# A retention layer and token mixer on one core: wq and wk in one product, named PSUM banks, weights later, a new order, smaller store descriptors

## The chip, the cores and the metric

One core of one Trainium2 chip. The metric is device time in microseconds of one execution. The kernel before had a median of 112.32 us in its first three runs (112.2 to 112.54).

A word on states: a run counts as slow when it is over 1.5% above the fastest of the same kernel in its group.

## The reference, cut to what matters

```python
# q, k, v: (4, 8, 768, 64) float32;  w_q, w_k: (512, 64);  w_out: (512, 512)
for t in range(S):                                   # retention, one state per head
    state = gamma * state + k[t] v[t]^T
    y[t] = q[t] . state / sqrt(D)
x = y.transpose(0, 2, 1, 3).reshape(B, S, 512)
W = (x @ w_q) @ (x @ w_k)^T / sqrt(64)               # token mixing without softmax
out = relu(W @ x) @ w_out                            # (4, 768, 512) float32
```

Both kernels cut the sequence into 12 pairs of 128-token chunks (three pairs per batch). Per pair: q and k are multiplied by powers of gamma (`cq`, `ck`), transposed (`trq`, `trk`), scores of two halves are made (`sc`), masked on the way out of PSUM (`eat`), multiplied by v (`ia`), and the inter-chunk part and the running state are added (`X`, `Y`, `st`). Then x is copied (`ex`), transposed (`xt`, `exT`) and multiplied by w_q and w_k (`wqk`). Once a batch's three pairs are there, z = wk^T x (`zm`), the mixing (`mx`), relu (`r`), the output product (`pj`), its copy (`eo`) and the store follow.

## The kernel before

A string gives the order of all steps; the letter names the engine of a copy (A ScalarE, V VectorE, P GpSimd). Each engine runs its own steps in that order.

```python
ORDER = """
fill.80 ck.0:V trk.0 cq.0:V ekT.0:A trq.0 cv.0:V fill.2 eqT.0:V
st.0 es.0.0:A sc.0.0 X.0 eat.0.0:V es.0.1:A sc.0.1 ck.1:P ia.0.0
# ... 39 more lines
"""
at_psum = pool("at_psum", 1, space=PSUM)   # 2 banks: one score tile at a time
y_psum = pool("y_psum", 1, space=PSUM)     # 2 banks
s_psum = pool("s_psum", 1, space=PSUM)     # 1 bank
psum = pool("psum", 3, space=PSUM)         # 3 banks for all else, in turn

for p in range(STAGES):                    # 6 pairs are asked for at the start
    for name in "kqv":
        load(name, p)
    if p == 2:                             # w_q, w_k and w_out (1 MB) behind pair 2
        ...
def wqk(e, p):
    for a in range(NDM):                   # wq, already transposed: 4 products of 256 columns
        nc.tensor.matmul(out=ps[:, 0 : 2 * C]..., lhsT=wq_sb[:, a]..., rhs=st["xT"][:, a]...)
    for c in range(2):
        for a in range(NDM):               # wk: 8 products of 64 columns
            nc.tensor.matmul(out=ps[:, 2 * C + c * DH : ...], lhsT=st["xT"][:, a, c, :], rhs=wk_sb[:, a, :])
```

## Time and profile before

| kernel before, profiled run | |
|---|---|
| span | 109.7 us (time 112.3) |
| TensorE busy, VectorE, ScalarE, GpSimd | 93.8, 64.9, 60.0, 49.4 us |
| start of the first real matmul, last matmul start | 8.7, 104.8 us |
| last output copy to end of span | 4.0 us |
| pauses of TensorE over 0.3 us between 8 us and the last matmul, in sum | 15.3 us |

"Pause" here and below is a distance over 0.3 us between the starts of two successive TensorE instructions, weight loads and matmuls counted alike, taken from the trace's list of instructions. The profile's "busy" row is not used for that, since matmul spans overlap (in the trace of the kernel before an output matmul lasts 380 ns in the mean, and the next one starts 216 ns after it). A position such as "before instruction 961" counts the same list from its start.

### The profile page before, as it was taken

How to read it: one execution, taken by the hardware profiler on the slowest of the kernel's cores; microseconds unless marked ns; L12 is line 12 of the kernel's file. 1: busy time of each engine (PE TensorE's matmuls, PEld its weight loads, DVE VectorE, ACT ScalarE, POOL GpSimd, SP SyncE). 2: the span in 40 equal slices, each digit the busy share in tenths (PEclk: the TensorE clock that was granted, in tenths of full speed). 3: DMA queues.
4: the chain of work that ended last, by engine and by line, in shares of the span. 5: the costliest groups of instructions: out<-in, count | busy, mean ns of one | idle time of the engine just before them, and what ended most of it. 6: DMA issues, size and time to landing. Idle time of an engine off the chain costs nothing.

```text
span 109.7 us, 4707 instructions
## 1 busy us (share of the span) xinstructions
PE 93.8 (85%) x2132; PEld 68.9 (63%) x2132; DVE 64.9 (59%) x87; ACT 60.0 (55%) x94; POOL 49.4 (45%) x41
## 2 busy tenths in 40 slices
PE   3999596994579899999998959999999999958930
PEld 3998485783458576667687837557787647633400
DVE  1066756894422665687688849799857954225100
ACT  5004137265273975958848515549587866554640
POOL 6405968008699996968229999321000000000000
PEclk9999958999967999999999999999999999999999
DMA  1999999999999999999999999824040022430471
GB/s 38 309 347 346 342 342 238 313 334 306 289 327 337 345 344 304 339 337 333 287 297 281 300 354 370 332 115 166 31 197 0 6 87 111 191 158 33 191 312 73
DMA packets 40917, 26.77 MB, mean 244 GB/s; under 512 B 1857, under 2 KB 38721, under 8 KB 40897
## 3 DMA queue, kind: packets, MB, share of 16 engines
q1 hardware_dynamic: 39856, 25.96, 75.0%
q10 hardware_dynamic: 1040, 0.52, 1.6%
q8 instruction: 16, 0.26, 0.9%
q14 instruction: 5, 0.03, 0.1%
HBM read 20.19 MB, written 6.29 MB: 241 GB/s over the span
## 4 chain that ended last, share of the span: by engine, by line
PE 78%; DVE 10%; issue 5%; ACT 3%; POOL 1%; POOLq 0%; DVEq 0%; ACTq 0%
PE o_ps L538 20%; PE at_ps L316 8%; PE y_ps L422 6%; PE ktr_ps L243 6%; PE xt_ps L445 6%; DVE at_sb L329 6%; PE wqk_ps L460 6%; PE qtr_ps L299 6%; PE y_ps L385 5%; PE ktr_ps L285 3%; PE z_ps L492 3%; PE wqk_ps L470 3%; PE mx_ps L514 3%; PE state_ps L385 2%; DVE xT L133 1%
## 5 line engine op out<-in xcount | busy, mean ns | idle before, releaser
L329 DVE TENSOR_TENSOR at_sb<-at_ps,cmask 128x1024 bf16<-128x1024 f32 x24 | 29.3, 1222 | 9.5 <-PE at_ps L316 9.3
L253 POOL TENSOR_TENSOR ks<-k_st,fk 128x1024 bf16<-128x1024 f32 x11 | 20.9, 1902 | 19.0 <-DMA k_st<-in_k_dram 14.8
L538 PE MATMUL o_ps<-wout_sb,relu 128*128 128x512 bf16 x96 | 24.1, 380 | 0.3 <-ACT o_st L132 0.3
L253 POOL TENSOR_TENSOR qs<-q_st,fq 128x1024 bf16<-128x1024 f32 x11 | 20.9, 1902 | 1.2 <-DMA q_st<-in_q_dram 1.2
L132 ACT COPY o_st<-o_ps 128x512 f32<-128x512 f32 x19 | 11.1, 586 | 9.9 <-PE o_ps L538 9.8
L316 PE MATMUL at_ps<-qT,kT 64*64 64x128 bf16 x384 | 10.6, 221 | 4.0 <-DVE at_sb L329 2.3
L538 PEld LDWEIGHTS <-relu 128*128 128x128 bf16 x96 | 8.2, 98 | 8.0 <-issue 1.2
L132 ACT COPY kT<-ktr_ps 128x1024 bf16<-128x1024 bf16 x7 | 7.1, 1015 | 9.9 <-PE ktr_ps L285 9.9
L529 ACT ACTIVATE relu<-mx_ps 128x512 bf16<-128x512 f32 x18 | 10.2, 598 | 3.3 <-PE mx_ps L514 2.6
L316 PEld LDWEIGHTS <-kT 64*64 64x64 bf16 x384 | 7.1, 106 | 6.7 <-issue 5.6
L132 ACT CAST s_sb<-state_ps 128x256 bf16<-128x256 f32 x16 | 6.0, 373 | 8.8 <-PE state_ps L385 8.7
L385 PE MATMUL y_ps<-s_sb,qT 64*64 64x64 bf16 x320 | 9.6, 195 | 1.0 <-DVE at_sb L329 1.0
L133 DVE COPY xT<-xt_ps 128x1024 bf16<-128x1024 bf16 x10 | 6.7, 686 | 6.1 <-PE xt_ps L445 6.1
L385 PEld LDWEIGHTS <-qT 64*64 64x64 bf16 x320 | 7.2, 108 | 4.7 <-issue 2.7
L385 PE MATMUL state_ps<-vs,ks 64*64 64x64 bf16 x320 | 8.9, 194 | 1.5 <-issue 1.4
L422 PE MATMUL y_ps<-vs,at_sb 64*128 64x64 bf16 x384 | 10.0, 193 | 0.2
L243 PEld LDWEIGHTS <-warm 128*128 128x128 bf16 x90 | 7.7, 129 | 1.9 <-DVE warm L174 1.1
L422 PEld LDWEIGHTS <-at_sb 64*128 64x128 bf16 x384 | 7.2, 96 | 2.6 <-DVE at_sb L329 0.5
L132 ACT CAST x_nat<-y_ps 128x1024 bf16<-128x1024 f32 x6 | 6.1, 1012 | 4.7 <-PE y_ps L422 4.6
L243 PE MATMUL ktr_ps<-identity,warm 128*128 128x128 bf16 x80 | 7.0, 275 | 1.9 <-POOL identity masks.py:199 1.9
L385 PEld LDWEIGHTS <-ks 64*64 64x64 bf16 x320 | 6.9, 109 | 2.4 <-issue 2.1
L531 DVE TENSOR_SCALAR relu<-mx_ps 128x512 bf16<-128x512 f32 x6 | 4.2, 692 | 7.1 <-PE mx_ps L514 7.1
(57 smaller groups left out, 137.5 us busy)
## 6 DMA issues: line engine op xcount, KB each, us to landing
q_st<-in_q_dram SPq DMA_DIRECT2D x12, 512.0 KB, 6.7
v_st<-in_v_dram SPq DMA_DIRECT2D x12, 512.0 KB, 6.5
k_st<-in_k_dram SPq DMA_DIRECT2D x11, 512.0 KB, 6.7
out_dram<-o_st SPq DMA_DIRECT2D x11, 512.0 KB, 2.7
wout_stage<-in_moe_w_out_dram SPq DMA_DIRECT2D x1, 1024.0 KB, 7.0
k_st<-in_k_dram ACTq DMA_DIRECT2D x1, 512.0 KB, 5.6
out_dram<-o_st SPq DMA_DIRECT2D x2, 256.0 KB, 2.8
wq_stage<-in_moe_w_q_dram SPq DMA_DIRECT2D x1, 128.0 KB, 5.4
```

What stands on the lines that cost most here:

```text
L132: return nc.scalar.copy(out=out, in_=in_)
L133: return ENGINES[e].tensor_copy(out=out, in_=in_)
L243: nc.tensor.transpose(dst, warm, identity)
L253: ENGINES[e].tensor_tensor(out=st[name + "s"].rearrange("p hp j x d -> p x (hp j) d"), in0=st[name + "_st"].rearrange("p (x hp) j d -> p x ...
L299: nc.tensor.transpose(ps[:, hp, :, j, :], st["qs"][:, hp, j], identity)
L316: nc.tensor.matmul(out=ps[rows(c), x, hi, j, :], lhsT=st["kT"][rows(x), hp, j, c, :], rhs=st["qT"][rows(x), hp, c, :], start=(hi == 0 and ...
L329: st["eat", half] = ENGINES[e].tensor_tensor(out=st["at", half].rearrange("p x hi j t -> p (x hi) (j t)"), in0=st["at_ps", half].rearrange ...
L385: out.append(nc.tensor.matmul(skip_group_check=True, **mm))
L422: nc.tensor.matmul(out=st["y_ps"][:, c, x, hp, :], lhsT=st["at", half][rows(c), x, hi, j, :], rhs=st["vs"][rows(c), hp, j, x, :], start=(( ...
L445: nc.tensor.transpose(ps[:, a, c, :], st["x"][:, c, a * 128 : (a + 1) * 128], identity)
L529: nc.scalar.activation(out=dst, in_=src, func=ACT.Relu)
L538: nc.tensor.matmul(out=ps, lhsT=st["relu"][:, a, j], rhs=wout_sb[:, a, :], start=(a == 0), stop=(a == NDM - 1),)
```

## The change

The intent: less TensorE work in `wqk`; two score tiles at once; pairs 3 to 5 earlier; no stores between loads; an order that fills TensorE's holes; and smaller packets, so that the core's instruction fetches are not held up behind large ones. The last purpose is my reading of it, and b_512b, below, does not bear it out. (The trace of the kernel before lists 16 packets of 16 KB on the instruction queue, q8, beside 4264 weight loads and matmuls: from that, and from the period of 256 in TensorE's stops, I take each packet to bring 256 instructions of TensorE.)

```diff
-for p in range(STAGES): ... load k, q, v; at p == 2: w_q, w_k, w_out
+LOADS = "q0 v0 k1 q1 v1 k2 q2 v2 w k3 q3 v3 k4 q4 v4 k5 q5 v5 o k6 ...".split()
+# k of pair 0 in two halves on two queues; stores only once every load has been issued
-            nc.sync.dma_start(out=dst, in_=pairs[p]["o"])
+            nc.sync.dma_start(out=dst, in_=pairs[p]["o"], max_dma_last_dim=512)
+                out=wout_stage, in_=moe_w_out.rearrange("(p a) m -> p a m", a=NDM), max_dma_last_dim=512
-    at_psum, y_psum, s_psum, psum = four pools
+    banks = psum.tile([128, 8, 512], FP32, name="banks")     # a step names its bank: sc.0.1@4
-    wqk: 4 products of 256 columns (wq) and 8 of 64 (wk)
+        for c in range(2):
+            for a in range(NDM):
+                nc.tensor.matmul(out=ps[:, c, :], lhsT=st["xT"][:, a, c, :], rhs=wqk_sb[:, a, :], ...)
+    ewq, ew: copy wq (twice, side by side) and wk out; tw: transpose wq; ewt: copy it out
-    r: two relus of 512 columns
+    r: one relu of 1024 columns over two banks
-    fill.80 ... (100 fillers of 128 columns)
+    fill.20@6 ... (32 fillers of 512 columns)
+# ORDER is new throughout, with more copies on VectorE; x is laid out so that w_q, w_k and w_out
+# can be loaded "(p a)" instead of "(a p)"
```

## The prediction

> **What bounds the kernel now.** I began with the page: busy times, then the slices.

> ```profile
> PE 93.8 (85%) x2132; PEld 68.9 (63%) x2132; DVE 64.9 (59%) x87; ACT 60.0 (55%) x94; POOL 49.4 (45%) x41
> ...
> PE   3999596994579899999998959999999999958930
> ...
> PEclk9999958999967999999999999999999999999999
> DMA  1999999999999999999999999824040022430471
> ```

> PE is busiest, and from slice 15 (about 40 us) it has hardly a hole. Before that it has holes, two dips of its clock, and a DMA queue that is full until 70 us. The table of busy time by window, cut where the character of the run changes, says the same in numbers (columns: window, its length, PE busy, weight loads, DVE, ACT, POOL, clock, DMA share, GB/s):

> ```profile
> 8.90:40.00 31.10, 24.88 (x629) 19.87 (x625) 18.16 (x21) 16.38 (x24) 22.64 (x14) 0.89 1.08 320
> 40.00:97.00 57.00, 55.20 (x1390) 39.24 (x1388) 41.06 (x50) 36.94 (x59) 23.73 (x14) 1.00 0.68 220
> 97.00:105.80 8.80, 6.69 (x38) 2.67 (x36) 2.77 (x4) 4.99 (x9) 0.00 (x0) 1.00 0.40 163
> ```

> Matmul spans overlap, so "busy" overstates the work. I took start-to-start distances of matmuls at full clock instead: 216 ns for an output matmul (512 columns), 56 for a 128-column transpose, 109 for the 256-column wq product, 29 for the 64-column wk product, 15 to 21 for the 64-row tiles. By counts: outputs 96 x 216 = 20.7 us, transposes 288 x 56 = 16.1, scores 8.1, at@v 7.5, inter and state 9.0, wq/wk 48 x 109 + 96 x 29 = 8.0, z 3.1, mx 3.8: **76.3 us**. From 8.9 to 105.2 us is 96.3. About 54 us of the work lies in 40:97, 7 after, so about 15 us in the 31 us from 8.9 to 40. That is where the time is lost.

> The chain of work that ended last shows how. At 24 us and again at 30 us (start, us, what):

> ```profile
> 25.38 0.29 PE at_ps L316 x11
> 25.67 1.40 issue
> 27.07 0.28 PE at_ps L316 x5
> 27.35 0.02 issue
> 27.37 1.24 DVE at_sb L329
> ...
> 30.54 0.84 PE xt_ps L445 x8
> 31.38 0.02 issue
> 31.40 0.70 DVE xT L133
> 32.10 0.04 issue
> 32.15 1.01 PE wqk_ps L460 x4
> ```

> Three losses are in view. (a) 1.40 us of "issue" in the middle of one score group, 11 of 16 matmuls done: no operand is missing. (b) One score buffer: `at_sb` takes 1.24 us on DVE, and the next score group must wait. (c) Eight transposes take 0.84 us where 0.45 is normal: half clock. The half clock lasted from 13.7 to 17.2 us and from 30.8 to 34.2.

> For (a) I counted the PE's instructions (weight loads and matmuls): it stops before number 961, 2497 and 2753, each 193 past a multiple of 256. An instruction packet of 16 KB ended 1.2 to 1.4 us before each resumption. The three stops cost 1.6 + 0.6 + 1.5 us. [...]the first while the output weights were in flight (2048-byte packets, 84 ns each; loads' 512-byte packets take 27 ns), the third just after the first store (4096-byte packets, 159 ns).

> [...]the two dips are 3.4 us long each, after thin PE work. [...]`at_sb` 1222 ns for 1024, `x_nat` 1221, against 686 for bf16 `xT`.

> ```profile
> L329 DVE TENSOR_TENSOR at_sb<-at_ps,cmask 128x1024 bf16<-128x1024 f32 x24 | 29.3, 1222 | 9.5 <-PE at_ps L316 9.3
> L253 POOL TENSOR_TENSOR ks<-k_st,fk 128x1024 bf16<-128x1024 f32 x11 | 20.9, 1902 | 19.0 <-DMA k_st<-in_k_dram 14.8
> ```

> The second row: POOL waited 14.8 us for loads of k, so the first third is fed by DMA, too.

> **The change part by part.**

> *wq and wk in one product.* 48 x 109 + 96 x 29 = 8.0 us becomes 96 matmuls of 128 columns and 24 transposes, 120 x 56 = 6.7 us: 1.3 us less PE. Evacuation grows from one copy of 384 columns (482 ACT, 555 DVE) to three, about 0.4 + 0.3 + 0.3 us; twelve times 0.5 is 6 us more on ACT and DVE, and one more round trip before mx, off the path except at the end.

> *Explicit banks.* Seven banks are shared by all; scores of one half go to one pair of banks while the other half is masked. Removes loss (b): at 11.1 to 14.1 us alone two `at_sb` of 1.24 us lay in series on the chain. relu becomes one instruction over two banks, about 1.0 us instead of 2 x 0.6.

> *Late weights.* Before, wq, wk and the 1 MB of w_out stand between pair 2 and pair 3. A load of 512 KB takes 1.5 us of the queue, so w_out 3.0: pairs 3 to 5 land 3 us earlier. Stores now come only after the last load; 20.2 MB at 0.34 MB/us end near 62 us rather than 70.

> *Fill.* 100 short filler matmuls become 32 of 512 columns, 20 of them in front: at half clock until about 6.9 us, they end at 8.2. k in halves is cast by then. So the first transpose starts as before (8.7).

> *New order.* I laid the order of each engine out by hand, token by token, up to the second half of pair 6's scores, with the durations above. Result: scores of pair 3 start near 27.4 us against 35.9 (with 1.5 us of z and wq/wk of batch 0 not yet done). At 45.5 us some 28.3 us of PE work are done. The kernel before reaches the same point near 52.4. **Lead 6.9 us**, in which 1.6 of the first fetch stop, 2.5 of half clock and 3 of w_out are contained.

> *Descriptors of 512 bytes.* If packets cause the late fetches, the two stops after 52 us (0.6 and 1.5, at 59.5 and 63.6) go: 2.0 less. Price: 8 x 84 = 0.67 becomes 32 x 27 = 0.86 us per engine for the last store, +0.2.

> *DVE.* Its list sums to 77 us (64.9 before; 24 masks alone 29.3), ACT to 56. By 45.5 us some 37 of these 77 are done, so 40 remain in about 50 us: dense, in order, beside a PE that has 46.7 in the same time. I charge 1.5 us.

> Sum: 112.3 - 6.9 - 0.8 (the rest of the 1.3 on PE) - 2.0 + 0.2 + 1.5 = **104.3 us**. The end itself (last copy 0.6, store 2.8, finish) stays.

> **The rivals.** First: *DVE becomes the bound*. For it: 77 us in about 95, its masks sit between every score and product. Against: ACT has room, and bank pairs let two scores wait. Every wait would turn up as PE idle behind `at_sb`; then the rest runs at 86% (as my layout of 27 to 45 us did), not 90: 107 to 108 us. Second: *instruction fetch bounds a faster PE*. For it: [...]the stop at 59.5 came with no store in flight. Stops then return before 62 us: 1 to 3 us, 106 us. Third: *the head is DMA-fed anyway* and the reorder waits for pairs instead of banks, or the PE goes thin and the clock halves again: gain only 3 in the head, 108 us. Fourth: all works, no DVE loss, order as good to the end: 101 us.

> **Range and chances.** The sum is 104.3; the fourth gives the low side, 100.5; the rivals singly reach 108, which I take as the high side. For "same" the change would have to lose nearly all of 8 us, two rivals together. Faster 0.92, same 0.06, slower 0.02.

> **What would show it.** Right: PE clock at full from about 7 us; scores of pair 3 near 28 us; no "issue" piece over 1 us in the chain after 20 us; PE work 75.0 by start-to-start; no score group waiting for `at_sb` in the first 30 us; the z product of batch 0 near 32 us; DVE near 77 busy; loads ending near 62. Wrong: stops at a fixed place modulo 256 still there (second rival), PE idle behind DVE growing between 45 and 97 us (first), half-clock slices (third), or PE starting later than 9.5 us because of the fillers.

## The result

105.81 us median of four runs (103.83, 104.13, 107.5, 108.59), the kernel before 112.43 in the same group. The ratio of the fast runs is **0.9233** (95% interval 0.9183 to 0.9282). Ratios are the mean time of one kernel's fast runs over that of the other's of the same rounds, so not quite the ratio of the medians quoted. Three later groups with the same kernel on other occasions gave medians of 106.51, 105.69 and 105.89 against 112.16, 111.52 and 112.02: ratios of medians 0.945 to 0.950. The means of their fast runs give 0.967, 0.950 and 0.944, but the first has only one fast run of the kernel before and the last only one of the changed kernel. The ratio of 0.9233 rests on two fast runs; about 5% is the better figure.

The page of the changed kernel, busy times and slices of 2.6 us (a run of the slow label, 105.8 us of span):

```profile
PE 90.7 (86%) x2040; PEld 63.3 (60%) x2040; DVE 77.0 (73%) x108; ACT 54.6 (52%) x87; POOL 46.1 (44%) x41
...
PE   5997986849999996998999699689999999999800
...
PEclk9999999975599999999999999999999999999996
DMA  1999998999999999999999999999133060661993
```

Its table by window, columns as in the prediction:

```profile
8.90:40.00 31.10, 26.99 (x759) 21.69 (x757) 23.93 (x34) 15.35 (x23) 20.21 (x14) 0.89 1.07 318
40.00:97.00 57.00, 52.84 (x1238) 37.01 (x1237) 46.10 (x58) 36.61 (x61) 21.78 (x13) 1.00 0.76 221
97.00:105.80 8.80, 3.23 (x15) 1.26 (x13) 2.99 (x4) 0.99 (x2) 0.00 (x0) 0.91 0.80 240
```

TensorE carries more in the first third (759 matmuls, some fillers among them, instead of 629) and *less* between 40 and 97 us (1238 instead of 1390, since much was done before); it is done about 5 us earlier. VectorE went up by the 12 us foreseen. The DMA queue is full (digits of 8 and 9) until 74 us, before until 71, and full again at the very end (two digits of 9), where before it was not (4 and 7). There is still a stretch of half clock (22.3 to 29.1 us).

Pauses of TensorE over 0.3 us, summed by stretch, in us, and the tail:

| profile | 8 to 30 | 30 to 50 | 50 to 70 | 70 to last matmul | last copy to end | span |
|---|---|---|---|---|---|---|
| before | 6.6 | 2.1 | 3.1 | 3.6 | 3.96 | 109.7 |
| after, first profile | 5.0 | 2.8 | 3.3 | 1.0 | 4.94 | 105.8 |
| after, again (fast label) | 4.3 | 3.6 | 3.0 | 0.6 | 4.95 | 104.7 |

So the time came from the head (about 2 us of pauses) and, unforeseen, from the last stretch (about 3 us); the middle, from 30 to 70 us, has about 1 us more of pauses than before; the tail (last copy to end) grew by 1.0 us. For the fast-label profile: the last matmul starts 6.0 us earlier (98.7 against 104.8); 3.8 of that are fewer pauses, 1.3 by estimate the smaller product, 0.9 the rest. In the rest are, not told apart, a first real matmul at 7.4 instead of 8.7 us and a half clock of 3.4 instead of 6.8 us. The longer tail takes 1.0 back: 5.0 us of span.

Two pauses of the changed kernel show what remains. The timeline of its first profile near 21 us (start, us, engine, line, operation, count, idle before):

```profile
20.57 0.35 PE L333 MATMUL banks<-qT,kT 64*64 64x128 bf16 x10
22.50 0.18 PEld L333 LDWEIGHTS <-kT 64*64 64x64 bf16 x6 [1.73 <-issue]
22.50 0.42 PE L333 MATMUL banks<-qT,kT 64*64 64x128 bf16 x6 [1.57 <-issue]
```

A score group stops after 10 of 16 matmuls, with no wait that the profile shows ("issue"). The stop stands before instruction 705 = 2 x 256 + 193, the same place modulo 256 as in the kernel before; "stop" below means a pause at this place. The half clock begins at 22.3 us, 0.2 us before the stop ends.

The other is at 14 us and is new. The same few instructions in the first profile, where it went well, and in the profile of a_same3, the same kernel, where it went badly:

```profile
13.68 0.68 DVE L127 CAST vs<-v_st 128x1024 bf16<-128x1024 f32 x1
...
14.21 1.91 POOL L263 TENSOR_TENSOR ks<-k_st,fk 128x1024 bf16<-128x1024 f32 x1 [1.05 <-DMA k_st<-in_k_dram]
```

```profile
14.00 1.90 POOL L263 TENSOR_TENSOR ks<-k_st,fk 128x1024 bf16<-128x1024 f32 x1 [0.49 <-DMA k_st<-in_k_dram]
14.02 2.43 DVE L127 CAST vs<-v_st 128x1024 bf16<-128x1024 f32 x1
...
16.50 0.26 PE L399 MATMUL banks<-vs,ks 64*64 64x64 bf16 x2 [1.93 <-DVE vs L127]
```

VectorE's cast of v of pair 1 took 0.68 us where it started before GpSimd's decay (by 0.53 us), and 2.43 us where it started 0.02 us after it; TensorE then waited 1.93 us for it, and the cast ended 0.55 us after GpSimd's operation. Why, the traces do not show. Ten profiles of the changed kernel and its variants have the two side by side. In four the cast starts first and takes 0.68 us, in six it starts 0.02 to 0.69 us later, takes 1.76 to 2.43 us and ends 0.55 us after GpSimd, in each of them. The kernel before had this cast on VectorE only for pair 0, while GpSimd was idle (686 ns). The clock in a_same3 is halved from 16.2 to 23.0 us; that begins in the last 0.35 us of the wait.

### The profile page after: what moved, and what is told of

It is laid out like the page before.

```text
span 105.8 us, 4560 instructions
## 1 busy us (share of the span) xinstructions
PE 90.7 (86%) x2040; PEld 63.3 (60%) x2040; DVE 77.0 (73%) x108; ACT 54.6 (52%) x87; POOL 46.1 (44%) x41
## 5 line engine op out<-in xcount | busy, mean ns | idle before, releaser
L345 DVE TENSOR_TENSOR at_sb<-banks,cmask 128x1024 bf16<-128x1024 f32 x24 | 28.9, 1220 | 7.6 <-PE banks L333 7.4
L263 POOL TENSOR_TENSOR ks<-k_st,fk 128x1024 bf16<-128x1024 f32 (+1 forms) x10 | 18.4, 1841 | 13.7 <-DMA k_st<-in_k_dram 6.5
L569 PE MATMUL banks<-wout_sb,relu 128*128 128x512 bf16 x96 | 23.0, 379 | 1.2 <-DVE wout_sb L127 1.0
L126 ACT CAST x_nat<-banks 128x1024 bf16<-128x1024 f32 x11 | 11.1, 1012 | 8.2 <-PE banks L399 7.4
L126 ACT COPY o_st<-banks 128x512 f32<-128x512 f32 x15 | 8.6, 589 | 9.0 <-PE banks L569 8.9
L333 PE MATMUL banks<-qT,kT 64*64 64x128 bf16 x384 | 10.6, 226 | 3.0 <-issue 1.6
L251 PE MATMUL banks<-warm 128*128 128x512 bf16 x32 | 10.2, 454 | 2.0 <-DVE warm L190 1.2
L399 PE MATMUL banks<-s_sb,qT 64*64 64x64 bf16 x320 | 10.1, 200 | 0.1
L399 PE MATMUL banks<-vs,ks 64*64 64x64 bf16 x320 | 8.8, 194 | 1.3 <-issue 1.1
L436 PE MATMUL banks<-vs,at_sb 64*128 64x64 bf16 x384 | 9.3, 195 | 0.2 <-DVE at_sb L345 0.2
```

The lines of the kernel that those rows point to most:

```text
L126: return nc.scalar.copy(out=out, in_=in_)
L251: nc.tensor.matmul(out=bank32(b), lhsT=warm[:, 0:128], rhs=warm, start=True, stop=True)
L263: ENGINES[e].tensor_tensor(out=st[name + "s"][:, :, :, xs].rearrange("p hp j x d -> p x (hp j) d"), in0=st[name + "_st"][:, xs].rearrange( ...
L333: nc.tensor.matmul(out=ps[rows(c), x, hi, j, :], lhsT=st["kT"][rows(x), hp, j, c, :], rhs=st["qT"][rows(x), hp, c, :], start=(hi == 0 and ...
L345: ENGINES[e].tensor_tensor(out=st["at", half].rearrange("p x hi j t -> p (x hi) (j t)"), in0=st["at_ps", half].rearrange("p (xhi jt) -> p ...
L399: out.append(nc.tensor.matmul(skip_group_check=True, **mm))
```

## The experiments

Twelve runs gave a result, in four groups; nine of them are variants, three the changed kernel again. In each group all kernels shared the runs of the kernel before on the same chip. Medians in us, with the ratio to the median of before:

| run | what | median | before | ratio of medians | stops at the 256-period, us in sum | tail |
|---|---|---|---|---|---|---|
| a_same | changed kernel | 106.51 | 112.16 | 0.950 | 7.7 | 4.95 |
| a_bigst | large stores | 105.37 | 112.16 | 0.940 | 5.2 | 4.33 |
| a_bigall | large stores and w_out | 108.16 | 112.16 | 0.964 | 6.4 | 4.35 |
| a_earlyw | w_out early | 106.48 | 112.16 | 0.949 | 2.3 | 4.95 |
| a_same2 | changed kernel | 105.69 | 111.52 | 0.948 | 6.1 | 4.94 |
| a_halfloads | half the loads | 103.46 | 111.52 | 0.928 | 3.4 | 4.69 |
| a_fly2 | two loads under way | 125.85 | 111.52 | 1.129 | see below | 4.91 |
| a_onescore | one score tile at a time | 109.26 | 111.52 | 0.980 | 2.2 | 4.95 |
| a_same3 | changed kernel | 105.89 | 112.02 | 0.945 | 3.6 | 4.94 |
| a_best | large stores, w_out cast moved | 106.21 | 112.02 | 0.948 | 4.6 | 4.32 |
| b_wqk | before, with one product | 112.57 | 112.02 | 1.005 | 3.7 | 3.97 |
| b_512b | before, with small descriptors | 109.99 | 112.01 | 0.982 | 3.9 | 4.10 |

"Stops at the 256-period" are pauses over 0.3 us before an instruction that lies 184 to 195 past a multiple of 256 (a few records are missing in some traces, which shifts the count by up to nine). Output matmuls at half clock that happen to lie there are not counted (1.2 us in a_bigall). The stops come from one profile each; the three unaltered profiles show 7.7, 6.1 and 3.6 (the first profile 5.4), so that a difference of 3 us between two kernels means nothing. What means something is *where* they can occur at all.

**The changed kernel again (a_same, a_same2, a_same3).**

> The changed kernel unaltered, as the yardstick for the other runs of this group, and in the hope of a profile in the fast state. Its first times were 103.8 and 104.1 us fast, 107.5 and 108.6 slow. Theory 1 (a fetch stop of TensorE in the thin part near 21 us, falling badly on the clock's windows, halves the clock for two windows): a fast profile shows the same stops at instruction numbers 193 past a multiple of 256, but one half-clock window of 3.4 us or none after 7 us, and a span near 102.2. Rival (slow runs have more or longer fetch stops): the fast profile lacks the stop before instruction 705 or has it under 0.5 us.

> The changed kernel unaltered, as the yardstick of this group. Earlier: ratio to the kernel before about 0.92 to 0.95 with a spread of some per cent. Expected again: stops of TensorE 192 instructions past multiples of 256, between 14 and 69 us, 5 to 6 us in sum, none after 70 us.

> The changed kernel unaltered, yardstick of this group: 0.92 to 0.95 of before; from the last copy to the end 4.9 to 5.0 us; w_out cast on VectorE 2.3 to 2.9 us with TensorE waiting 1.0 to 1.6 us for it.

The fast-label profile of the first (104.7 us) has *more* stops than the slow one, seven in 7.7 us, but only one half-clock window (22.1 to 25.5 us) instead of two; its span is 104.7 us, not the expected 102.2. So neither view alone orders the runs; the rival (slow runs have more stops) does not hold for this pair, and the theory holds for it only. In a_same2 and a_same3 the long pause is the wait for v at 14 us, not a stop; each has its half clock from 16.2 us on, for 3.4 and 6.8 us. The third expectation on w_out was wrong for these runs: the cast on VectorE took 1.22 or 1.23 us in a_same, a_same2 and a_same3, and 2.33 us only in the first profile, where GpSimd had begun 0.66 us before it.

**Stores, and w_out, in large descriptors (a_bigst, a_bigall).**

```diff
-            nc.sync.dma_start(out=dst, in_=pairs[p]["o"], max_dma_last_dim=512)
+            nc.sync.dma_start(out=dst, in_=pairs[p]["o"])
# a_bigall: the same for w_out
```

> The stores' 512-byte limit taken off (4096 bytes, the last two 2048), w_out left at 512. Theory 1 (512-byte stores only lengthen the queue at the end, where five stores of 512 KB stand in a row, and do not help the fetches): about 0.7 to 1.5 us faster than the changed kernel, the last copy to the end of the span 4.0 instead of 5.0 us, stops of TensorE as before. Rival (large packets delay fetches): one stop more or longer after 55 us, and 1 to 2 us slower.

> Both limits taken off (stores 4096, w_out 2048 bytes or more per descriptor). Theory 1 (packet size doesn't matter to fetches): same as the run with large stores alone, within 0.5 us. Rival: the fetch that falls into the w_out transfer (about 31 to 36 us) comes late and gives a stop of over 1 us there, 1 us slower than with large stores alone.

The tail is the clean part: 4.33 and 4.35 us from the last copy to the end, against 4.94 or 4.95 in all four profiles with 512 bytes and the same final steps. **0.6 us** are the price of the small store packets here, where the last stores stand in a row; in the kernel before the same packets cost 0.13 us (b_512b, 4.10 against 3.97). (A 4096-byte packet took 159 ns in the trace of the kernel before, eight of 512 bytes 8 x 27 = 216.) The stores' own time to landing, from the page's DMA issues of a_same and then a_bigst:

```profile
out_dram<-o_st SPq DMA_DIRECT2D x2, 256.0 KB, 3.3
```

```profile
out_dram<-o_st SPq DMA_DIRECT2D x2, 256.0 KB, 2.7
```

The stops did not grow with large stores (one profile: nothing over 0.4 us at the period after 50 us). With w_out large as well there is a stop of 1.74 us at 37.8 us, as the rival had it; but the unaltered a_same has one of 0.96 us at 36.8 us, and the runs of a_bigall range from 102.26 to 109.75 us: its median is 2.8 us above that of a_bigst, its one fast run the fastest of the group. Its longest stop, 2.35 us at 69 us, lies far from w_out. That part is **inconclusive**.

**w_out early (a_earlyw).**

```diff
-LOADS = "... k2 q2 v2 w k3 q3 v3 k4 q4 v4 k5 q5 v5 o k6 ..."
+LOADS = "... k2 q2 v2 w o k3 q3 v3 k4 q4 v4 k5 q5 v5 k6 ..."
```

> w_out asked for right after wq and wk, as before the change, instead of after pair 5. Theory 1 (the head is fed by DMA): pairs 3 to 5 land 3 us later, scores of pair 3 some 2 to 3 us later, and the whole 2 to 3 us slower. Rival (the head is bound by chains and masks, so the delay is absorbed): under 1 us slower.

106.48 against 106.51: no difference in the medians (only one run of a_earlyw is labelled fast, 104.65). The edit did what it should: k, q and v of pairs 3 to 5 landed 2.5 to 3.3 us later than in a_same. Yet scores of pair 3 start at 29.5 us, unaltered at 28.5 to 30.7. No gain from the later weights shows: the rival holds.

**Half the loads (a_halfloads).** Its output is wrong, which doesn't matter for the time.

```diff
+        if p >= NG // 2:                       # pairs 6 to 11 reuse the staged tiles of 0 to 5
+            st[name + "_st"] = pairs[p - NG // 2][name + "_st"]
+            return
```

> Wrong result on purpose: q, k and v of pairs 6 to 11 are not loaded; the staged tiles of pairs 0 to 5 are used again. All engines' work stays, the loads end near 34 us instead of 62. Theory 1 (stops come wherever loads keep the DMA rings full, whatever the packet size): no stop at a multiple of 256 after about 37 us, where there were some 3 us of them; 2.5 to 4 us faster than unaltered. Rival A (stops come from TensorE's own pace): stops stay, same time within 1 us. Rival B (DVE is the bound from 40 us on): stops go but the time falls by under 1 us.

After 33 us there is not one stop at the period; in a_same2, of the same group, there are six after 37 us (0.37, 0.35, 0.82, 1.39, 1.16 and 0.98 us). The window 40 to 70 us of a_halfloads and then of a_same2:

```profile
40.00:70.00 30.00, 28.41 (x774) 21.09 (x773) 27.13 (x34) 23.03 (x35) 19.33 (x11) 1.00 0.25 74
```

```profile
40.00:70.00 30.00, 26.33 (x668) 18.87 (x667) 23.00 (x29) 21.41 (x32) 22.35 (x13) 1.00 1.04 306
```

With the queue at 74 GB/s instead of 306, TensorE does 774 matmuls instead of 668. Instruction 1985 is reached at the same time (47.9 and 48.1 us), instruction 3009 3.4 us earlier (66.2, 69.6). The ratio of the fast runs is 0.9309 (0.9211 to 0.9408), of a_same2 0.9504 (0.944 to 0.9568): 2.2 us of 111.5, a little under what was expected. VectorE is not the bound there: it does 27.1 us of work in those 30, and the only waits of TensorE over 0.3 us for it are one behind the cast of w_out, which ends at 41.3 us, and one of 0.5 us. The time of the run cannot separate the stops from the waits for late q, k and v, which go with the same loads. The traces can in part: after 33 us no pause over 0.3 us of a_same2 waits for a load or for a cast of one; 5.1 us of them are stops.

The packets of the traces show the lateness itself. In every profile of the twelve runs and of both kernels, an instruction packet starts about when TensorE begins the 256 instructions before those that it brings (at most 0.5 us earlier), or later; how much later follows the loads. In a_same2 the delay is 1.9 to 3.9 us up to 71.5 us, and 0.1 to 0.7 us between 74 and 84 us; in a_halfloads 2.4 to 3.8 us up to 35.3 us, and 0.0 to 1.0 us between 38 and 81 us. Small packets did not shorten it: while loads ran it was 1.2 to 4.2 us in the kernel before, and about 0.9 to 4.1 us in b_512b, below; but the longest of all, 5.2 us, stands beside the large w_out packets of a_bigall. That the fetch is late while the DMA queue is full is thus measured (1.9 to 3.9 us in a_same2, with a DMA share of 1.04 between 40 and 70 us; 0.0 to 1.0 us in a_halfloads from 38 us on, with 0.25), and not only inferred from stops.

**At most two loads under way (a_fly2).**

```diff
+        if len(loads) >= 2:
+            tc.add_manual_dep(dma.ins, loads[-2].ins.name, ...)
+        loads.append(dma)
```

> At most two loads of q, k, v under way at a time (each waits for the landing of the one before the last) where there were four or so. Theory 1a[...]: stops shrink from 5 to 6 us to under 2 us, loads land as early within 1 us; 2 to 4 us faster. Theory 1b[...]: DMA share and stops stay, the time within 1 us or slower by the gaps in the loads.

125.85 us. Two loads are too few: 195 to 262 GB/s in most slices, the last load landed at 93.0 us instead of 68 to 70, and long waits for k and q. At the 256-period there is one pause of 0.31 us, and one of 2.98 us that waits for k. So stops nearly vanish below a full queue, but this is no way to use it. Neither 1a nor 1b as stated: the loads did not land as early.

**One score tile at a time (a_onescore).**

```diff
+                        if hi == j == x == c == 0 and eats:
+                            tc.add_manual_dep(mm.ins, eats[-1].ins.name, ...)   # the last mask before it
# and five sc steps stand behind that eat in ORDER
```

> Score groups no longer overlap with the masking of the one before: each score group waits for the last mask ahead of it, and five score groups move behind that mask in the order; banks and all else stay. Theory 1 (two score groups at once were a main part of the gain): 3 to 6 us slower than unaltered, TensorE idle behind the masks in the first 45 us. Rival (the new order and late weights gave the lead, and the masks are hidden by other work): under 1.5 us slower.

109.26 against 105.69 us: 3.6 us slower by the medians, without an interval; five of its six runs carry the slow label, and its one fast run, 106.08, is 1.0 us above the fastest of a_same2 and 0.7 us above the mean of its four fast runs. The waits of this run, in us in total, times, longest:

```profile
PEld L341 <- DVE at_sb L362: 7.2, 8, 1.7
PE banks L341 <- DVE at_sb L362: 5.5, 6, 1.6
```

No score group waits for a mask in a_same2's list of waits. The loss against a_same2 is 1.6 us at instruction 234, 2.2 at 1985 and 2.8 at 3521, but at 705 the two are level, since a_same2 waited 2.1 us for v in between. That two score tiles save waits is shown; their share of the gain lies between about 1 us (fast runs) and 3.6 us (medians), so that "a main part" is not shown.

**The kernel before with one product for wq and wk (b_wqk).**

```diff
-    4 products of 256 columns and 8 of 64, one copy
+    8 products of 128 columns, two copies, two transposes two steps later, one copy
```

> The kernel before with only wq and wk in one product, the transposes two TensorE steps after the copies, banks and order else as before. Theory 1 (1.3 us less on TensorE, but one more turn in three shared banks and 6 us more copies): within 1.5 per cent of before, either way. Rival (the product alone gives a good part of the gain): 2 to 4 us faster.

112.57 against 112.02: no gain alone, as theory 1 had it (two fast runs on each side: means 110.8 and 109.6).

**The kernel before with small descriptors (b_512b).** A first form did not build (the four-dimensional w_out view cannot be cut further); here w_out is four loads.

```diff
-            nc.sync.dma_start(out=dst, in_=pairs[p]["o"])
+            nc.sync.dma_start(out=dst, in_=pairs[p]["o"], max_dma_last_dim=512)
# and w_out in four loads of 512-byte descriptors
```

> The kernel before with only the descriptor sizes of the change: stores at 512 bytes, w_out in four loads of 512-byte descriptors. Theory 1 (packet size does not set the fetch stops; 512-byte stores only lengthen the end): stops of TensorE at multiples of 256 plus 193 remain, 2 to 5 us in sum while loads run, last copy to end 0.2 to 0.6 us longer, time within 1 per cent of before. Rival (as in the prediction: small packets let fetches in time): at most one stop over 0.5 us, 1.5 to 3 us faster.

Stops before instructions 193 (or 184 to 187, records missing) past a multiple of 256: 0.57, 1.41, 1.27 and 0.63 us, 3.9 in sum, against 4.1 before the change of descriptors. Two of them in the chain that ended last:

```profile
56.83 0.34 PE z_ps L495 x3
57.17 1.14 issue
58.31 0.73 PE z_ps L495 x9
...
61.91 0.15 PE state_ps L388 x9
62.06 1.07 issue
63.13 0.21 PE state_ps L388
```

They did not go. The one beside w_out shrank from 1.61 to 0.57, but the one that stood beside the first large store is still 1.27 us. The last, at 74 us, lies beside stores. The ratio of the fast runs is 0.994 (0.980 to 1.008). Small packets do not keep the fetches in time; a small effect beside w_out stays open.

**Large stores, and the cast of w_out on ScalarE (a_best).**

```diff
-... sc.5.0@4 WO:V es.4.1:A ...        LOADS: ... v5 o k6
+... ez.0:A WO:A eat.4.1:V ...         LOADS: ... v4 o k5
# and stores as in a_bigst
```

> The changed kernel with stores in large descriptors again, the cast of w_out on ScalarE right after the first z instead of on VectorE ahead of the first output product, and w_out loaded one pair earlier. Expected: the end 0.6 us shorter (4.3 us from last copy to end), the wait of TensorE for the w_out cast (1.0 to 1.6 us near 41 us) gone, together 1.0 to 2.5 us faster than unaltered. Rival (the wait only moves on to the masks behind it, VectorE being dense): 0.6 us, the end alone.

106.21 against 105.89 us: nothing gained, although the tail is 4.32 us, the cast takes 1.90 us on ScalarE at 36.3 us, and no TensorE wait for it is left. Its pauses between 50 and 70 us fell to 1.85 us, and yet instruction 3009 is reached at 69.2 us, hardly before the unaltered kernel (69.5 to 70.0). My first reading was that TensorE waits for the last loads whatever it gains before: the cast of pair 11's q starts at 68.5 us, unaltered at 67.5 to 68.4. The trace does not show this: no pause over 0.3 us of TensorE between 60 and 70 us waits for a load or its cast. a_best takes 9.9 us from instruction 2497 to 3009 (unaltered 10.2 to 11.0), but it comes to 2497 at 59.2 us (unaltered 58.5 to 59.8), so it had come there late; why stays open. No version was found that beats the changed kernel for certain; a_bigst is 0.7 us better by the means of its fast runs (105.3 against 106.0), which is about the tail.

## Why the prediction was right

It said 104.3 us (100.5 to 108.0); the first group gave 103.8 and 104.1 in fast runs and a median of 105.81, later groups about 106. Right in sum, partly by luck: some of its errors cancel.

- **Lead in the head: mis-sized.** The prediction put the lead at 6.9 us, with the transposes of pair 5's x at 45.5 us against an equivalent point of 52.4 before. They start at 46.9 to 48.5 us: a lead of 3.9 to 5.5. The first real matmul came at 7.4 to 7.9 us and not at 8.7, so the start was better than foreseen. My layout by hand knew neither the stops at 15 to 23 us (up to 2.1 us each) nor the slow cast of v (1.9 us of TensorE), nor the half clock beside either (from 22.3 us at the stop in the first profile, from 16.2 us at the cast in a_same3). "PE clock at full from about 7 us" was wrong in every profile.
- **Late weights, 3 us: wrong.** a_earlyw shows none.
- **The two stops after 52 us go, 2.0 us: wrong.** This is the step that failed as to its mechanism. The stops stay (second rival), with small packets in either kernel (a_same, b_512b), and they go where the loads go (a_halfloads). The evidence that I had, the first stop beside w_out and the third beside the first store, was a coincidence with a full queue. The trace of the kernel before could have told: the last large packet of w_out ended at 22.6 us, and the late instruction packet started at 24.8; TensorE had begun the 256 instructions before those that it brings 4.2 us earlier, at 20.6 us.
- **The end itself stays, +0.2: wrong in both directions.** The tail grew by 1.0 us: 0.6 by the small packets; the other 0.4 stays with large packets too (4.33 against 3.96), I think because stores stand in a row, which no run tested. But the pauses before it, 3.6 us after 70 us in the kernel before, fell to 0.6 to 1.0. The waits of over 0.3 us for the last z, relu and output copies, in the kernel before 2.1 us in sum, are gone; by my reading because the new order keeps output products in hand while the last z and mixing are made. I had not counted those pauses as something that the order could fill.
- **VectorE, +1.5: the sum was right (77 expected, 77.0 measured), the wait was not.** Masks hold TensorE back little (no score group of a_same2 waits for one); casts out of SBUF beside GpSimd do (2.1 us there), which the prediction did not see.
- **Loads end near 62 us: wrong.** The last one lands at 68.2 to 69.8 us, as in the kernel before (69.0); the queue moved about 300 to 320 and not 340 GB/s, and the issuing engine waited for casts to free staged tiles (5.7 us for GpSimd's casts of q alone). The third rival had this in part.
- **The smaller product, 1.3 us:** the counts are as said (120 matmuls of 56 ns at the median). Alone it gives nothing (b_wqk), presumably as its copies and turns in the banks take it back; within the new banks it may count, which no run shows.

From the transposes of pair 5's x to the last matmul the prediction implied 51.1 us (52.4 - 0.8 - 2.0 + 1.5); measured are 51.2 to 52.3. The 2.0 for the stops is false there, and the 2 to 3 us of the last stretch stand in its place.

What stays open: why the delay of a fetch differs from one execution to the next, and what it waits for while loads run; what share of the 2.2 us of a_halfloads is stops and what is late data too short to show as a pause; and how much of the gain belongs to the order alone, since no run has the old order with the new banks.

## What to carry to other kernels

Look at the position of unexplained pauses in an engine's instruction list before blaming a neighbour in time: a fixed remainder modulo 256 named this cause, taking the load away tested it where changing packet sizes did not move it, and the start of each instruction packet against TensorE's place in its list measures it without any run. Do not put a VectorE cast from SBUF where it can start beside a long GpSimd operation on the critical path; here a lead of 0.02 us decided over 1.75 us (0.68 against 2.43). And give the last stores large packets: small ones cost 0.6 us of tail in the changed kernel and 0.13 us in the kernel before. That the last stores should also find an empty queue is my guess, which no run tested. The tail is the one term that comes out the same, within 0.03 us, in every profile with the same last steps, store sizes and loads.
